# R loaded for two chunks at once and turned on TensorE into fp32, V and scaled A in one transposing transfer, and a new order of the work

## The chip, the cores and the metric

The kernel runs on one core of a Trainium2 chip. A core has a matrix engine (PE, TensorE, with a weight-load path PEld), a vector engine (DVE, VectorE), a scalar engine (ACT, ScalarE), a general engine (POOL, GpSimd), a queue that mostly issues transfers (SP, SyncE), and 16 DMA engines that all queues share. Operands lie in SBUF, results of PE in the banks of PSUM. The engines run side by side, each through its own instructions in program order, and wait for one another by semaphores. The metric is the time of one execution on the device in microseconds (us); less is better.

## The reference

Two layers. First a recurrence over 768 tokens for 4 x 8 heads of width 40, with a state of 40 x 40 for each head:

```python
for t in range(S):
    y[:, :, t] = np.einsum('bhd,bhde->bhe', rt, state)
    Sa = np.einsum('bhde,bhe->bhd', state, at)
    state_decay = state * wt[:, :, None, :] - np.einsum('bhd,bhe->bhde', Sa, bt)
    state = state_decay + np.einsum('bhd,bhe->bhde', vt, kt)
```

Then a feed-forward layer on the 3072 rows of 320 numbers that `y` makes: `h = x @ w_in` (320 x 2048), `g = max(h, 0) ** 2`, `out = g @ w_out` (2048 x 320). All inputs and the output are fp32.

## The kernel before, in words

**Tiling.** The 768 tokens are cut into 6 chunks of 128. One chunk of one sequence is a *batch*: 24 batches, number m = 4 x chunk + sequence, each with 128 tokens on the partitions and 8 heads x 40 columns. A batch has two *steps* of 4 heads (48 steps). Within a chunk the recurrence is written as matrix products: the decays are summed up (logarithm, a product with a triangle of ones, exponentials), K and B are divided by the summed decay, A is multiplied by it, and 128 x 128 products of tokens with tokens, masked to the past, take the place of the loop over tokens. A state (the tile UZ) goes from chunk to chunk. The feed-forward layer runs in 48 units over half-chunks (or, at both ends, over single batches) as their rows of `y` are done.

**Tokens of work.** The program is a string `ORDER` of some 1,900 tokens, one after the other; each names a function and a number, and often the engine (`:A` ACT, `:D` DVE, `:P` POOL) or the PSUM bank (`@f`). The order of the tokens is the order of issue on every engine and queue. The ones that matter here:

- `lW`, `lK`, `lB`, `lA`, `lV`, `lR` (`load`, L82 to L87): one input of one batch, 128 x 8 runs of 160 bytes, on SP's queue. R and V of a batch share a tile NRV; there are four such buffers (L64, L65).
- `ln`, `cs`, `cx`, `xi`, `gp`: the decays (L166 to L190). `pk` and `pa` (L201, L206) scale K and B, and A, into a padded bf16 tile of three planes, KBAp. `cv` (L210) casts R and V into a padded tile RVp. `gw` (L197) and `gl` make the chunk's last decay.
- *Turning*: products need K, B, A, R and V with the head's columns on the partitions. For batches 0 to 7 PE turns R and V (`rm`, L223, 8 transposes into a bf16 bank) and `rv` (L226) copies 1024 values of each partition out; `ta` and `at` do so for A. For batches 0 to 19 `kt` and `kv` turn K and B on PE. From batch 8 on, `rt` (L229) is a transposing transfer of R and V, and `ka` (L253) one of A (batches 8 to 19) or of K, B and A (20 to 23), all from SP's queue. Their targets are the tiles RV (four buffers) and KBT.
- `a` (L280): tokens-by-tokens products of K and B with A, in two halves of the array, into two banks; `av0`, `av1` mask them into CN. `p`, `m`, `k1`, `c`, `k2`, `s`: the correction of the recurrence. `t`, `tv`: the turned correction TB. `e` (L402): the products with R (from the tiles RV and TB); `ev0`, `ev1` mask them into EX. Where ACT evicts, POOL cuts the mask afterwards (`aq`, `eq`, L305).
- `z`, `kb` (L430, L444): `y` and the new state in one bank; `y` and `u` evict them. `xt`, `xv` turn `y` for the feed-forward layer. `x`, `jk`, `en` are sums for a check of the range (general code, not run on these inputs, stands behind it).
- `fr`, `fa`, `fb`: a unit's first product (L542); `ra`, `rb` relu on ACT (L562); `q` squares (L568); `o1`, `o2` the second product (L577); `ov`, `ow` evict and store.
- `wt`, `wd`, `wo`: the weights, from POOL's queue (`wd` on SP's). `f`, `i`: constants and zeros. `w` (`warm`, L134): filler products of 128 x 128 ones on PE, 26 for `w.0` and 8 for each other, 16 of the 19 in the first chunks and three at the end.

The queue of SP carries all loads, the transposing transfers and the stores in the string's order, and waits in line wherever one of them must wait.

## Time and profile before

| | |
|---|---|
| median of 3 runs | 257.62 us (256.45 to 258.14) |
| profiled execution, its own time | 259.12 us |
| its span, first to last instruction | 257.3 us |
| granted TensorE clock, mean | 0.993 |
| instructions | 9803 |
| transfers' packets | 184468, of these 180064 under 512 bytes |
| HBM read, written | 28.84 MB, 3.93 MB |

The page of the profile gives busy time by engine, the span in slices, the queues, the chain of waits that ended last (followed back from the last instruction), and groups of instructions by line. A windows view gives the busy time of each engine in a stretch. A matmul's duration in a group is from its start to its modelled end (some 220 ns for 128 columns); matmuls overlap, so the pace of a row of them is read from the chain, where eight turnings take 0.45 us. `hp`, `ca`, `ex`, `uy`, `tt`, `P`, `op_` are PSUM tiles, `hs`, `CN`, `EX`, `KBT`, `RV` tiles of SBUF.

### The profile page before, as it was taken

The numbers are of one execution on the slowest core, as the hardware profiler recorded it, in microseconds if no ns is written. First come the engines' busy times: TensorE is split into PE (matmuls) and PEld (weight loads), VectorE is DVE, ScalarE is ACT, GpSimd is POOL, SyncE is SP. The second block draws the span as 40 slices with busy tenths as digits, with TensorE's granted clock in tenths as the row PEclk, the third lists the DMA queues.
The fourth block names the chain that finished last, engine by engine and source line by source line (L and its number), as shares of the span: only waits on it lengthen the run. The fifth ranks groups of instructions, "written<-read, shape, count | busy, mean of one in ns | idle before, by whom it ended". The sixth has DMA issues, their size and how long they took to land.

```text
span 257.3 us, 9803 instructions
## 1 busy us (share of the span) xinstructions
PE 241.3 (94%) x4020; PEld 201.8 (78%) x4020; DVE 202.4 (79%) x429; ACT 205.9 (80%) x470; POOL 203.0 (79%) x231
## 2 busy tenths in 40 slices
PE   8897867999999999999999999999999997999993
PEld 7776656989888888788888788888878885787872
DVE  3887877899999889898798898879798986664440
ACT  3567989589989988978999887889989876869811
POOL 6487987779989979999998999897896993397110
PEclk9999999799999999999999999999999999999999
DMA  7999999999988989999999999989999989470011
GB/s 127 182 151 153 169 176 168 170 167 167 162 162 137 157 151 182 137 178 180 157 159 184 159 167 172 167 162 185 141 187 180 178 167 148 97 120 28 28 57 59
DMA packets 184468, 38.46 MB, mean 149 GB/s; under 512 B 180064, under 2 KB 183136, under 8 KB 184416
## 3 DMA queue, kind: packets, MB, share of 16 engines
q1 hardware_dynamic: 183072, 35.14, 80.9%
q0 software_dynamic: 1344, 2.62, 6.4%
q8 instruction: 33, 0.54, 0.9%
q14 instruction: 19, 0.16, 0.2%
HBM read 28.84 MB, written 3.93 MB: 127 GB/s over the span
## 4 chain that ended last, share of the span: by engine, by line
PE 58%; POOL 13%; DMA 12%; SPq 8%; ACT 4%; issue 2%; DVE 1%; POOLq 0%; ACTq 0%
PE hp L542 17%; SPq L85 8%; DMA NKB<-in_b_dram 6%; PE tt L218 3%; PE cs L173 3%; PE ca L287 3%; PE ex L410 3%; POOL Gt L568 3%; PE uy L456 3%; DMA NRV<-in_r_dram 2%; DMA KBT<-KBAp 2%; POOL KBAp L202 2%; PE uy L451 2%; PE P L344 2%; POOL CN L307 2%
## 5 line engine op out<-in xcount | busy, mean ns | idle before, releaser
L542 PE MATMUL hp<-XS,WIN 128*128 128x256 bf16 (+3 forms) x720 | 73.3, 255 | 0.0
L562 ACT ACTIVATE hs<-hp 128x512 bf16<-128x512 f32 x96 | 55.6, 600 | 14.5 <-PE hp L542 13.2
L542 PEld LDWEIGHTS <-WIN 128*128 128x128 bf16 (+1 forms) x720 | 49.6, 115 | 6.1 <-issue 3.6
L302 DVE TENSOR_TENSOR CN<-ca,MEX 128x512 bf16<-128x512 f32 x60 | 39.5, 683 | 8.6 <-PE ca L287 8.0
L577 PEld LDWEIGHTS <-Gt 128*128 128x128 bf16 x384 | 35.1, 97 | 12.2 <-issue 0.3
L302 DVE TENSOR_TENSOR EX<-ex,MEX 128x512 bf16<-128x512 f32 x60 | 39.8, 683 | 4.4 <-PE ex L410 4.3
L568 POOL TENSOR_TENSOR Gt<-hs 128x1024 bf16<-128x1024 bf16 x21 | 40.4, 1927 | 0.6 <-ACT hs L562 0.3
L307 POOL TENSOR_SCALAR_AFFINE_SELECT CN<-CN 128x512 bf16<-128x512 bf16 x36 | 25.1, 703 | 10.0 <-ACT CN L300 7.8
L307 POOL TENSOR_SCALAR_AFFINE_SELECT EX<-EX 128x512 bf16<-128x512 bf16 x36 | 25.0, 711 | 5.9 <-ACT EX L300 3.9
L198 POOL TENSOR_TENSOR Gp<-NW,GP 32x320 bf16<-32x320 f32 x20 | 17.6, 886 | 11.3 <-DVE osb L157 7.6
L568 DVE TENSOR_TENSOR Gt<-hs 128x1024 bf16<-128x1024 bf16 x27 | 21.7, 810 | 5.8 <-ACT hs L562 4.3
L365 ACT ACTIVATE jk<-CN 128x1024 bf16<-128x1024 bf16 x24 | 25.7, 1071 | 0.2
L300 ACT ACTIVATE CN<-ca 128x512 bf16<-128x512 f32 x36 | 21.0, 594 | 4.7 <-PE ca L287 4.5
L202 POOL TENSOR_TENSOR KBAp<-NKB,GI 128x640 bf16<-128x640 f32 x14 | 21.6, 1545 | 3.2 <-DMA NKB<-in_b_dram 2.5
L300 ACT ACTIVATE EX<-ex 128x512 bf16<-128x512 f32 x36 | 20.5, 597 | 2.8 <-PE ex L410 1.9
L287 PE MATMUL ca<-KBT 64*128 64x128 bf16 x384 | 18.2, 221 | 3.7 <-DMA KBT<-KBAp 1.7
L361 POOL TENSOR_TENSOR Cc<-x,SN 128x320 bf16<-128x320 f32 x24 | 20.1, 836 | 1.9
L456 PE MATMUL uy<-KBAp,EX 128*128 128x40 bf16 x384 | 21.3, 181 | 0.0
L207 POOL TENSOR_TENSOR KBAp<-NA,GP 128x320 bf16<-128x320 f32 x18 | 16.3, 907 | 5.6 <-DMA NA<-in_a_dram 2.9
L360 POOL TENSOR_TENSOR x<-Mc,c 128x320 f32<-128x320 bf16 x24 | 20.5, 854 | 0.3
L472 DVE TENSOR_TENSOR YN<-uy,GP 128x224 bf16<-128x224 f32 (+1 forms) x48 | 16.5, 346 | 4.4 <-PE uy L456 4.4
L456 PEld LDWEIGHTS <-EX 128*128 128x128 bf16 x384 | 17.9, 96 | 0.9 <-issue 0.3
(151 smaller groups left out, 623.0 us busy)
## 6 DMA issues: line engine op xcount, KB each, us to landing
NW<-in_w_dram SPq DMA_DIRECT2D x24, 160.0 KB, 3.8
NA<-in_a_dram SPq DMA_DIRECT2D x24, 160.0 KB, 4.0
NKB<-in_k_dram SPq DMA_DIRECT2D x24, 160.0 KB, 3.9
NKB<-in_b_dram SPq DMA_DIRECT2D x24, 160.0 KB, 4.3
NRV<-in_v_dram SPq DMA_DIRECT2D x24, 160.0 KB, 4.0
NRV<-in_r_dram SPq DMA_DIRECT2D x24, 160.0 KB, 3.9
out_dram<-osb SPq DMA_DIRECT2D x24, 160.0 KB, 3.4
WOUT<-in_moe_w_out_dram POOLq DMA_DIRECT2D x2, 640.0 KB, 6.6
```

Source lines behind the costliest of these rows:

```text
L85: nc.sync.dma_start(out=natural(pair, m)[:, u], in_=nat_srcs[key][bb, :, c * L:(c + 1) * L, :].rearrange("h t e -> t h e"))
L202: engine("pk", m).tensor_tensor(out=bt[m].KB[:, 0:2, :, 0:D], in0=nat.pop(("KB", m))[:], op=ALU.mult, in1=bt[m].GI[:].rearrange("p (u h) e ...
L287: nc.tensor.matmul(out=ca[s][:, i, u, :], lhsT=o.KBT[half(s), u, j0 + i, :], rhs=o.KBT[half(s), 2, j0 + i, :], start=(i == 0 and u == 0), ...
L300: nc.scalar.activation(out=out, in_=in_[:], func=ACTF.Copy)
L302: nc.vector.tensor_tensor(out=out, in0=in_[:], op=ALU.mult, in1=MEX[:].rearrange("p (i u) x -> p i u x", u=2))
L307: nc.gpsimd.affine_select(out=t_, in_=t_, pattern=[[0, 2], [0, 2], [1, L]], compare_op=ALU.is_gt, fill=0.0, base=0, channel_multiplier=-1)
L365: nc.scalar.activation(out=jk[:], in_=CNs[m, "b"][:].rearrange("p x i s u t -> p (x i s) u t")[:, :, 1, :], func=ACTF.Square, accum_out=AC ...
L456: nc.tensor.matmul(out=uy[:, (2 * i + s) * D:(2 * i + s + 1) * D], lhsT=EXs[st][:, i, s, u, :], rhs=o.KB[:, u, 2 * (j0 + i) + s, 0:D], sta ...
L542: nc.tensor.matmul(out=o.hp[u][:, i], lhsT=inner(g, rows, j), rhs=XSs[o.c][rows, g, o.bs, :], start=(o.begun[u] == 1), stop=(o.begun[u] > ...
L562: nc.scalar.activation(out=o.hs[:, u], func=ACTF.Relu, in_=o.hp[u][:].rearrange("p j a b -> p (j a b)"))
L568: engine("q", n).tensor_tensor(out=o.Gt[:, o.j0:o.j0 + 2 * o.per].rearrange("p j a b -> p (j a b)"), in0=hs, in1=hs, op=ALU.mult)
L577: nc.tensor.matmul(out=ops[n][:], rhs=WOUT[:, j, :], lhsT=Gts[h][:, b_, j, :] if h in SPLIT else Gts[h][:, j, b_, :], start=(j == 0), stop ...
```

## The change

- **R for two chunks.** Where the string has a `cr` token (batches 0 to 3 and 8 to 11), `lR` of these loads 256 tokens: partition p gets the tokens 2p and 2p+1 of two chunks, 128 x 8 runs of 320 bytes. `lR` of batches 4 to 7 and 12 to 15 is gone: 16 `lR` in place of 24. `cr` casts both chunks' R into plane 0 of two padded tiles, and `cv` of batches 0 to 15 casts V alone.
- **R turned on PE into fp32.** `rn` (16 tokens, batches 0 to 15) multiplies four 128 x 128 blocks with the identity into an fp32 bank, and `rv` (16) copies 512 fp32 values of each partition out and puts the even and odd tokens in order, into planes 0 and 3 of a tile RVT that now has four planes; plane 3 is the R of the odd chunk (`turned_r`). Batch m turns half of the heads for both chunks, batch m+4 the other half. `rm` is gone.
- **V and scaled A.** `pa` now writes plane 2 of the tile RVA (R, V, A) and not the tile of K and B. In batches 0 to 7 V is turned on PE alone (`vm`, four transposes; `vv` copies 512 bf16 values); A as before. In batches 8 to 15 one transposing transfer `rt` turns V and A together. In batches 16 to 19 `rt` turns R and V and a new `aa` A; in 20 to 23 there are `rt` (R, V), `aa` (A) and `ka` (K, B).
- **Fillers.** `warm` issues products of 512 columns, 7 for `w.0` and 2 for each other.
- **Order.** The whole string is written anew, 1937 tokens in place of 1909, with other engines for many of them. Counts that change: `q` 27 on DVE and 21 on POOL become 23 and 25; `pa` 6 on DVE and 18 on POOL become 8 and 16; `gw` 4 and 20 become 6 and 18; `pk` 10 and 14 become 11 and 13; `m` 15 on ACT and 9 on DVE become 11 and 13; `ov` 8 and 14 become 12 and 10; `s` 18 and 6 become 20 and 4; `kv` 6 and 14 become 8 and 12; `tv` 6 and 18 become 4 and 20; `at` 3 and 5 become 6 and 2; masks 72 on ACT and 120 on DVE become 70 and 122; `cv` 13 on ACT, 2 on DVE and 9 on POOL become 10, 4 and 10; `cr` 2, 1 and 5; `rv` 4 on ACT and 4 on DVE become 9 and 7; `vv` 5 and 3.

The diff, without the rest of the order and the table of tokens:

```diff
@@ -76,15 +76,25 @@
 
     def natural(key, m):
         if (key, m) not in nat:
-            nat[key, m] = natp.tile([128, len(key), NHH, D], FP32, name=f"N{key}", tag=f"N{key}")
+            tag = "NRV" if key == "RR" else f"N{key}"
+            nat[key, m] = natp.tile([128, len(key), NHH, D], FP32, name=tag, tag=tag)
         return nat[key, m]
+
+    def paired(m):
+        return ("cr", m - m // NB % 2 * NB) in pick
 
     def load(key, m):
         pair, u = SHARED.get(key, (key, 0))
         c, bb = divmod(m, NB)
-        nc.sync.dma_start(
-            out=natural(pair, m)[:, u],
-            in_=nat_srcs[key][bb, :, c * L:(c + 1) * L, :].rearrange("h t e -> t h e"))
+        if key == "R" and paired(m):
+            nc.sync.dma_start(
+                out=natural("RR", m)[:].rearrange("p a h e -> p (a h e)").rearrange(
+                    "p (h x) -> p h x", h=NHH),
+                in_=r[bb, :, c * L:(c + 2) * L, :].rearrange("h (p a) e -> p h (a e)", a=2))
+        else:
+            nc.sync.dma_start(
+                out=natural(pair, m)[:, u],
+                in_=nat_srcs[key][bb, :, c * L:(c + 1) * L, :].rearrange("h t e -> t h e"))
 
     NHC = 2 * NCH
     AN, AM, AC, AG, AI = 0, NBC, NBC + NHC, NBC + 2 * NHC, 2 * NBC + 2 * NHC
@@ -97,8 +107,10 @@
     MEX = gl.tile([128, 4, L], BF16, name="MEX")
     HM = gl.tile([128, 1, 2], BF16, name="HM")
     pads = {key: [gl.tile([128, len(key), NHH, 64], BF16, name=f"{key}p{i}") for i in range(n)]
-            for key, n in (("KBA", 4), ("G", 3), ("RV", 4))}
-    RVs = [gl.tile([128, 2, PB, L], BF16, name=f"RV{i}") for i in range(4)]
+            for key, n in (("KB", 4), ("G", 3))}
+    RVAs = gl.tile([128, 4, 3, NHH, 64], BF16, name="RVAp")
+    pads["RVA"] = [RVAs[:, i] for i in range(4)]
+    RVs = [gl.tile([128, 4, PB, L], BF16, name=f"RV{i}") for i in range(4)]
     SNs = [gl.tile([128, PB, 2, 64], BF16, name=f"SN{i}") for i in range(NSN)]
     UZs = [gl.tile([128, NP, 128], BF16, name=f"UZ{i}") for i in range(2)]
     YNs = [gl.tile([128, NG * 128], BF16, name=f"YN{i}") for i in range(3)]
@@ -114,7 +126,7 @@
             for u in range(2):
                 eng.memset(HM[64 * u:64 * u + 64, :, u:u + 1], 1.0)
         elif k < 16:
-            key, i = (("KBA", k - 5) if k < 9 else ("G", k - 9) if k < 12 else ("RV", k - 12))
+            key, i = (("KB", k - 5) if k < 9 else ("G", k - 9) if k < 12 else ("RVA", k - 12))
             eng.memset(pads[key][i][:] if key == "G" else pads[key][i][:, :, :, D:64], 0.0)
         elif k < 19:
             eng.memset(SNs[k - 16][:, :, :, D:64], 0.0)
@@ -131,10 +143,11 @@
     def bank(x, k, i=0):
         return HOME[pick[x, k][1][i]]
 
-    def warm(k, n=8):
-        wu = ps.tile([128, 128], FP32, name="wu", **bank("w", k))
-        for i in range(26 if k == 0 else n):
-            nc.tensor.matmul(out=wu[:], lhsT=ones_b[:], rhs=ones_b[:], start=True, stop=True)
+    def warm(k, n=2):
+        wu = ps.tile([128, 4, 128], FP32, name="wu", **bank("w", k))
+        for i in range(7 if k == 0 else n):
+            nc.tensor.matmul(out=wu[:], lhsT=ones_b[:], start=True, stop=True,
+                             rhs=ones_b[:].rearrange("p (u x) -> p u x", u=1).to_broadcast([128, 4, 128]))
 
     def half(s):
         return slice(64 * s, 64 * s + 64)
@@ -160,8 +173,13 @@
 
     def home(m):
         o = bt[m] = Batch()
-        o.G, o.KB, o.RV = (pads[key][m % len(pads[key])] for key in ("G", "KBA", "RV"))
+        o.G, o.KB, o.RV = (pads[key][m % len(pads[key])] for key in ("G", "KB", "RVA"))
         o.RVT, o.YN = RVs[m % 4], YNs[m % 3]
+        c, bb = divmod(m, NB)
+        o.both = bt[m - NB].both if c % 2 else Batch()
+        o.turned_r = lambda j: o.RVT[:, 3 if paired(m) and c % 2 else 0, j, :]
+        if c % 2 == 0:
+            o.both.pad = RVAs[:, 2 * (bb % 2):2 * (bb % 2) + 2, 0]
 
     def b_ln(m):
         bt[m].lnW = ffp.tile([128, NHH * D], FP32, name="lnW", tag="lnW", bufs=2)
@@ -204,11 +222,17 @@
             in1=bt[m].GI[:].rearrange("p (u h) e -> p u h e", u=1).to_broadcast([128, 2, NHH, D]))
 
     def b_pa(m):
-        engine("pa", m).tensor_tensor(out=bt[m].KB[:, 2, :, 0:D], in0=nat.pop(("A", m))[:, 0],
+        engine("pa", m).tensor_tensor(out=bt[m].RV[:, 2, :, 0:D], in0=nat.pop(("A", m))[:, 0],
                                       in1=bt[m].GP[:], op=ALU.mult)
 
     def b_cv(m):
-        move(pick["cv", m][0], bt[m].RV[:, :, :, 0:D], nat.pop(("RV", m))[:])
+        lo = 1 if paired(m) else 0
+        move(pick["cv", m][0], bt[m].RV[:, lo:2, :, 0:D], nat.pop(("RV", m))[:, lo:2])
+
+    def b_cr(m):
+        move(pick["cr", m][0], bt[m].both.pad[:, :, :, 0:D],
+             nat.pop(("RR", m))[:].rearrange("p a h e -> p (a h e)").rearrange(
+                 "p (h a e) -> p a h e", a=2, h=NHH))
 
     def turned(pad, us=(0, 1), t_=None, **place):
         if t_ is None:
@@ -220,17 +244,40 @@
                     in_=pad[:, u, 2 * j:2 * j + 2, :].rearrange("p a b -> p (a b)"))
         return t_
 
-    def b_rm(m):
-        bt[m].t1 = turned(bt[m].RV, **bank("rm", m))
+    def b_rn(m):
+        o, j0 = bt[m], 2 * (m // NB % 2)
+        o.t1 = ps.tile([128, 2, 2, L], FP32, name="tt", **bank("rn", m))
+        for j in range(2):
+            for a_ in range(2):
+                nc.tensor.matmul(
+                    out=o.t1[:, j, a_], rhs=IDb[:], start=True, stop=True, skip_group_check=True,
+                    lhsT=o.both.pad[:, a_, 2 * (j0 + j):2 * (j0 + j) + 2, :].rearrange(
+                        "p a b -> p (a b)"))
 
     def b_rv(m):
-        move(pick["rv", m][0], bt[m].RVT[:], bt[m].t1[:])
-
-    def b_rt(m):
+        o, j0 = bt[m], 2 * (m // NB % 2)
+        move(pick["rv", m][0],
+             o.RVT[:, 0:4:3, j0:j0 + 2, :].rearrange("p c j (t a) -> p j c t a", a=2),
+             o.t1[:].rearrange("p j a (c t) -> p j c t a", c=2))
+
+    def b_vm(m):
+        bt[m].t4 = turned(bt[m].RV, us=(1,), **bank("vm", m))
+
+    def b_vv(m):
+        move(pick["vv", m][0], bt[m].RVT[:, 1], bt[m].t4[:, 0])
+
+    def turn_by_transfer(m, lo, hi):
         o = bt[m]
         nc.sync.dma_start_transpose(
-            out=o.RVT[:].rearrange("p u j t -> p (u j) t"),
-            in_=o.RV[:].rearrange("p u h e -> p (u h e)"))
+            out=o.RVT[:, lo:hi].rearrange("p u j t -> p (u j) t"),
+            in_=o.RV[:, lo:hi].rearrange("p u h e -> p (u h e)"))
+
+    def b_rt(m):
+        lo = 0 if not paired(m) else 2 if ("vm", m) in pick else 1
+        turn_by_transfer(m, lo, 2 if ("aa", m) in pick or ("ta", m) in pick else 3)
+
+    def b_aa(m):
+        turn_by_transfer(m, 2, 3)
 
     def b_kt(m):
         bt[m].t2 = turned(bt[m].KB, **bank("kt", m))
@@ -238,23 +285,22 @@
     def kbt(m):
         o = bt[m]
         if not hasattr(o, "KBT"):
-            o.KBT = chp.tile([128, 3, PB, L], BF16, name="KBT", tag="KBT", bufs=4)
+            o.KBT = chp.tile([128, 2, PB, L], BF16, name="KBT", tag="KBT", bufs=4)
         return o.KBT
 
     def b_kv(m):
-        move(pick["kv", m][0], kbt(m)[:, 0:2], bt[m].t2[:])
+        move(pick["kv", m][0], kbt(m)[:], bt[m].t2[:])
 
     def b_ta(m):
-        bt[m].t3 = turned(bt[m].KB, us=(2,), **bank("ta", m))
+        bt[m].t3 = turned(bt[m].RV, us=(2,), **bank("ta", m))
 
     def b_at(m):
-        move(pick["at", m][0], kbt(m)[:, 2], bt[m].t3[:, 0])
+        move(pick["at", m][0], bt[m].RVT[:, 2], bt[m].t3[:, 0])
 
     def b_ka(m):
-        o, lo = bt[m], 2 if ("kt", m) in pick else 0
         nc.sync.dma_start_transpose(
-            out=kbt(m)[:, lo:3].rearrange("p u j t -> p (u j) t"),
-            in_=o.KB[:, lo:3].rearrange("p u h e -> p (u h e)"))
+            out=kbt(m)[:].rearrange("p u j t -> p (u j) t"),
+            in_=bt[m].KB[:].rearrange("p u h e -> p (u h e)"))
 
     def last_decay(m, uy, at):
         o = bt[m]
@@ -285,7 +331,7 @@
             for i in range(2):
                 for s in range(2):
                     nc.tensor.matmul(out=ca[s][:, i, u, :], lhsT=o.KBT[half(s), u, j0 + i, :],
-                                     rhs=o.KBT[half(s), 2, j0 + i, :], start=(i == 0 and u == 0),
+                                     rhs=o.RVT[half(s), 2, j0 + i, :], start=(i == 0 and u == 0),
                                      stop=True, skip_group_check=True)
 
     def st_a_ev(st, s):
@@ -324,7 +370,7 @@
         P = Ps[m] = ps.tile([128, PB, 2, 64], FP32, name="P", **bank("p", m))
         if c > 0:
             for j in range(PB):
-                nc.tensor.matmul(out=P[:, j, :, 0:D], lhsT=o.KBT[:, 2, j, :],
+                nc.tensor.matmul(out=P[:, j, :, 0:D], lhsT=o.RVT[:, 2, j, :],
                                  rhs=heads(UZ[:, PB * bb + j, :]), start=(j == 0), stop=False,
                                  skip_group_check=True)
         for h in range(NHH):
@@ -408,7 +454,7 @@
                 for s in range(2):
                     lhsT = SnT[half(s), j0 + i, :] if u else o.RVT[half(s), 1, j0 + i, :]
                     nc.tensor.matmul(out=ex[s][:, i, u, :], lhsT=lhsT,
-                                     rhs=o.RVT[half(s), 0, j0 + i, :],
+                                     rhs=o.turned_r(j0 + i)[half(s)],
                                      start=(i == 0 and u == 0), stop=True, skip_group_check=True)
 
     EXs = {}
@@ -432,7 +478,7 @@
         uy = uys[st] = ps.tile([128, 8 * D + PB], FP32, name="uy", **bank("z", st))
         if c > 0:
             for i in range(2):
-                nc.tensor.matmul(out=cols(uy, 2 * i * D), lhsT=o.RVT[:, 0, j0 + i, :],
+                nc.tensor.matmul(out=cols(uy, 2 * i * D), lhsT=o.turned_r(j0 + i),
                                  rhs=heads(TBs[st // 2 - NB + LAG][:, PB + j0 + i, :]), start=(i == 0), stop=False,
                                  skip_group_check=True)
             for i in range(2 if c + 1 < NCH else 0):
@@ -622,150 +668,153 @@
     SPLIT = (0, 1, 11)
     ORDER = """
-        f.1:D lW.0 f.2:P lA.0 w.4@x w.11@0 f.4:D lW.1 f.20:D f.0:D f.9:D w.8@u lK.0 ln.0 f.16:D
...
+        lW.0 lK.0 f.0:D f.13:D f.1:P w.13@1 ln.0 w.2@u f.3:D lW.1 f.14:P f.17:P f.20:D lV.0 f.5:D
...
     """
```

291 lines of the change are left out of this document (147 added, 144 removed).

## The prediction

> **What bounds the kernel now.** First the page's totals, then the stages, then the chain, then the groups. The page:
> ```profile
> PE 241.3 (94%) x4020; PEld 201.8 (78%) x4020; DVE 202.4 (79%) x429; ACT 205.9 (80%) x470; POOL 203.0 (79%) x231
> DMA  7999999999988989999999999989999989470011
> q1 hardware_dynamic: 183072, 35.14, 80.9%
> PE 58%; POOL 13%; DMA 12%; SPq 8%; ACT 4%; issue 2%; DVE 1%; POOLq 0%; ACTq 0%
> ```
> No engine is far ahead of the others, and the row of the 16 DMA engines reads 9 for most of the time. So an average decides nothing; the stages do (bounds; length, then busy us of PE, PEld, DVE, ACT, POOL; clock, DMA share, GB/s):
> ```profile
> 0.00:48.00 48.00, 39.02 (x678) 33.01 (x679) 36.52 (x84) 33.98 (x74) 34.79 (x56) 0.99 0.96 161
> 48.00:128.00 80.00, 79.91 (x1427) 68.32 (x1425) 71.78 (x149) 71.24 (x167) 74.31 (x80) 0.99 0.98 162
> 128.00:216.00 88.00, 87.01 (x1447) 72.11 (x1444) 75.94 (x158) 76.81 (x179) 78.19 (x81) 1.00 1.00 170
> 216.00:257.30 41.30, 35.38 (x480) 28.32 (x478) 18.17 (x42) 23.84 (x51) 15.75 (x17) 1.00 0.35 68
> 208.00:224.00 16.00, 14.16 (x226) 11.32 (x224) 10.75 (x21) 11.76 (x26) 7.68 (x10) 1.00 0.81 140
> ```
> The reader sees three regimes. Up to 48 us the DMA engines are full (0.96) while PE, whose 39.02 us hold fillers too, has gaps: the start waits for data. From 48 to 216 us PE is busy for 166.92 of 168 us with the DMA engines at 0.98 to 1.00 beside it: PE sets the pace, DMA is a close second, and DVE, ACT and POOL have 6 to 12 us to spare in each of the two stages. From 216 us PE runs nearly alone. The chain of waits shows where DMA still decides (start, length, what):
> ```profile
> 27.16 5.75 DMA NRV<-in_r_dram
> ...
> 36.12 7.58 DMA NKB<-in_b_dram
> 43.72 1.20 DVE KBAp L202
> 44.97 0.62 PE tt L218 x8
> ...
> 74.49 1.09 PE op__1912 L577 x8
> 75.91 0.45 PE tt L218 x8
> ...
> 131.54 3.66 DMA NKB<-in_b_dram
> 135.62 1.55 POOL KBAp L202
> ...
> 152.26 1.56 POOL KBAp L202
> 153.86 0.62 PE tt L218 x8
> ...
> 213.73 5.37 DMA KBT<-KBAp
> 219.54 0.50 PE uy L456 x16
> ```
> The start ends with batch 5's b and its turning. At 131.5 us a late b puts POOL behind, and the chain stays on POOL until 153.8. At 213.7 us the last chunk's scaled K and B leave for the transposing transfer late, and `a` waits for it.
>
> **The change part by part.** Prices, first of one instruction, from the groups kept apart by form (busy us, mean ns of one, idle before):
> ```profile
> L218 PE MATMUL tt<-IDb,RVp 128*128 128x128 bf16 x64 | 4.9, 219 | 0.1
> L137 PE MATMUL wu<-ones_b 128*128 128x128 bf16 x170 | 13.5, 242 | 1.1 <-DVE HM L113 1.1
> L153 ACT ACTIVATE RVp<-NRV 128x640 bf16<-128x640 f32 x13 | 9.6, 739 | 3.0 <-DMA NRV<-in_r_dram 3.0
> L155 POOL CAST RVp<-NRV 128x640 bf16<-128x640 f32 x9 | 6.8, 753 | 3.8 <-DMA NRV<-in_r_dram 2.5 <-PE cs L173 1.2
> L153 ACT ACTIVATE RV<-tt 128x1024 bf16<-128x1024 bf16 x4 | 4.1, 1019 | 0.0
> L157 DVE COPY RV<-tt 128x1024 bf16<-128x1024 bf16 x4 | 2.7, 680 | 0.0
> L157 DVE COPY KBT<-tt 128x512 bf16<-128x512 bf16 x5 | 2.1, 419 | 1.0 <-PE tt L218 1.0
> L153 ACT ACTIVATE KBT<-tt 128x512 bf16<-128x512 bf16 x3 | 1.8, 595 | 1.6 <-PE tt L218 1.6
> L302 DVE TENSOR_TENSOR EX<-ex,MEX 128x512 bf16<-128x512 f32 x60 | 39.8, 683 | 4.4 <-PE ex L410 4.3
> L300 ACT ACTIVATE EX<-ex 128x512 bf16<-128x512 f32 x36 | 20.5, 597 | 2.8 <-PE ex L410 1.9 <-issue 0.8
> L568 POOL TENSOR_TENSOR Gt<-hs 128x1024 bf16<-128x1024 bf16 x21 | 40.4, 1927 | 0.6 <-ACT hs L562 0.3
> L568 DVE TENSOR_TENSOR Gt<-hs 128x1024 bf16<-128x1024 bf16 x27 | 21.7, 810 | 5.8 <-ACT hs L562 4.3 <-issue 1.5
> ```
> Then of one issue on SP's queue, from the views of the tiles NRV, RV and KBT (min/median/max ns):
> ```profile
> L85 SPq DMA_DIRECT2D NRV<-in_r_dram x24: 429/638/1142, 9.8 to 218.9; - x24
> L231 SPq DMA_TRANSPOSE RV<-RVp x16: 1232/1378/2762, 85.8 to 224.9; - x16
> L255 SPq DMA_TRANSPOSE KBT<-KBAp x16: 1192/1417/2886, 72.5 to 213.7; - x16
> ```
> *PE.* `rm` goes: 8 batches of 8 turnings (the 64 of the first row). `vm` brings 8 x 4 and `rn` 16 x 4, together 96, so 32 more. The chain (at 75.91) gives 0.45 us for eight in a row, 56 ns each: **+1.8 us**, none of it in batches 0 to 7 (64 against 64), all in 8 to 15, where PE is the bound, so it counts in full. Bounds: 0 if it falls into PE's small waits, and 32 x 219 ns = 7.0 us if nothing overlaps; I take 1.8, because such turnings come in fours and eights. The fillers go from 170 of 128 columns to 43 of 512: 21,760 columns against 22,016, no change in time, and they fill waits.
>
> *Evictions.* Before, `rv` is 4 x 1.019 us on ACT and 4 x 0.680 on DVE. After, `rv` moves 512 fp32 values of each partition 16 times (9 on ACT, 7 on DVE) and `vv` 512 bf16 values 8 times (5 and 3). By the rows for such sizes: ACT 9 x 0.597 + 5 x 0.595 - 4.1 = +4.2, DVE 7 x 0.683 + 3 x 0.419 - 2.7 = +3.3. `rv` reads PSUM with a step of 128 and writes pairs; no row has that. Bounds: the bf16 rate (0.42 on DVE) and twice the fp32 rate (1.37); I take the fp32 rows, the nearest in size and type.
> The Trainium skill ("VectorE: DVE Perf Modes", section "Why PSUM operands drop a tier") speaks against fp32 here: VectorE reads fp32 from PSUM at single rate only, where bf16 may go at double rate. The rows bear it out (680 ns for 1024 bf16 values, 683 for 512 fp32). With bf16 the seven would cost 2.9 us and not 4.8, by this trace; off PE's path, either leaves the sum as it is.
>
> *Casts.* `cv` halves in 16 batches and `cr` takes the other half in 8 of double width: the same elements and 8 more instructions. A half cast costs between half and all of a whole one, so 0 to 16 x 0.37 = 6 us over three engines; I take 1, near the lower end, since halving a copy brings 680 ns to 419. With that and the letters that the new order gives (`q` on POOL 21 to 25 at 1.927 against 0.810 on DVE; `pa`, `gw`, `pk` the other way; `m`, `s`, `kv`, `tv`, `at`, `ov` between ACT and DVE), token for token by such rows, ACT has about 3, DVE 5 and POOL 3 us more than before. Their cover is the 6 to 12 us of each stage above: taken as **0**. If the cover is gone, each of these us counts, up to 5.
>
> *DMA and SP's queue.* 183,072 packets at 80.9% of 16 engines' 257.3 us are 18.2 ns each; a load of 128 x 8 runs is 1.16 us of all 16. Sixteen loads of R become eight with as many runs each, of 320 bytes. A run of double size costs between one and two of today's, so the eight save between 0 and 9.3 us; I take the middle, 4.6. In transposing transfers, batches 8 to 15 go from V, R and A in two to V and A in one; 16 to 19 keep two; 20 to 23 go from two to three (`rt`, `aa`, `ka`). That is 32 to 28 issues and 56 to 48 planes; taking 1,024 packets for each of the 144 loads and 128 for each of the 24 results, some 580 packets are left for a plane, so 8 planes are 5.3 us. DMA falls by about 10 us of 208, SP's queue by 8 x 0.64 + 4 x 1.4 = 10.7 us.
> The Trainium skill ("DMA: Bandwidth & Descriptors", section "Why small descriptors are slow (HBM only)") gives each packet a fixed 3 cycles beside one for every 32 bytes; by that rule (an estimate) 320 bytes cost 13 and two of 160 cost 16, so R would save 3.5 us and not 4.6.
> As PE is the pace from 48 us, the lighter queues buy only what DMA still ends:
> - Start: by the order, 35 loads stand ahead of `fr.0` before and after, but four of them are double: 0 to +4.7 us. Ahead of batch 5's `kt.5` they are 39 and 37: -2.3 to +2.3. In chunk 0 come four more `rn`, `rv` and the wide `cr`, on engines with 11 to 14 us free of 48. I take **+0.5**.
> - 131 to 154 us: the chain runs over POOL behind a b that was awaited 3.66 us. With SP's queue and DMA lighter by then, I take **-1.5** (0 to -3.7).
> - 208 to 224 us: PE does 14.16 of 16. The order now issues K and B of batch 23 over 90 places earlier, and `pk`, `pa` of 23 run on DVE. Late next is `aa.23` behind `ka.23` on SP, which stands 24 places ahead of `a.46` as `ka.23` did. For the 1.84 us that PE lacks, and a little of the small waits around, I take **-2.0** (0 to -5.4, the whole wait).
> - A new wait: `rt` of 8 to 15 waits for the cast of V and for scaled A, and behind it on SP stand loads and results. V gets later, A not; `e` needs V only after `a` needs A. **0**, bounds 0 to +3 (two issues of 1.4).
> - End: in the last units `q` runs on POOL (44, 45, 47: 1.93 against 0.81), beside seven lots of `o` of 1.09 us each on PE (the chain at 74.49): **0**, up to +1.1.
> Sum: 1.8 + 0.5 - 1.5 - 2.0 = -1.2 us. The profiled execution is 259.12 us with a span of 257.3, and 1.5 above the median of 257.62; so 257.9 for such an execution, and **256.4** beside the median.
>
> **The rivals.** About 1% (2.6 us) is what a measurement of this kernel can tell from no change.
> 1. The relief counts more. POOL has 78.19 of 88 us and leads the chain for 18 us after 135.6; DMA is at 1.00. If the late data of the middle and of the end go wholly, it is 257.6 + 1.8 - 3.7 - 5.4 = 250.4 with the rest at 0; halfway to there from the forecast is **253.4**. For it: DMA and SP are both lightened before 128 us. Against: PE is busy 79.91 of 80 where that happens.
> 2. The start shortens: two loads fewer ahead of `kt.5` save 2.3 us, or the dip of the clock goes, which the two rows below show: 0.04 and 0.07 of 16 us, 1.8 us. With one of them, 257.6 + 1.8 - 3.5 - 2.1 = **253.8**. Against: the double loads.
> ```profile
> 32.00:48.00 16.00, 12.11 (x263) 10.66 (x262) 13.01 (x32) 12.42 (x23) 11.57 (x18) 0.96 0.99 170
> 48.00:64.00 16.00, 16.00 (x334) 14.69 (x333) 14.57 (x31) 14.02 (x33) 13.84 (x16) 0.93 0.99 169
> ```
> 3. Slower, at the start: R for two chunks must be there, cast, turned and evicted before the first `e`. Where DMA is full, four double loads cost up to 4.7 us and four more evictions of some 0.65 in turn half of their 2.6, which later stages, bound by PE, cannot give back. It decides if the loads ahead of `fr.0` end last: 257.6 + 1.8 + 4.7 + 1.3 - 3.5 = **261.9**. Against: loads of chunk 1 are fewer by four.
> 4. Slower, evictions: ACT, DVE and POOL get 3 to 5 us each. If a bank is evicted late in the middle because `rv` stands ahead of a mask or a relu, PE waits: 257.6 + 1.8 + 5 - 3 (the other three terms) = **261.4**. It decides when the stage's DVE exceeds about 76 of 80 us.
> 5. It saves nothing that ends last: all transfers were hidden; PE's 1.8 stays, **259.4**.
>
> **How the numbers follow.** Forecast 256.4 (its own range 255.1 to 258.8) 0.27; rival 1 0.22; rival 2 0.10; rival 3 0.19; rival 4 0.14; rival 5 0.08. Faster by over 1% (below 255.0) is 1 and 2: 0.32. Within 1% is the forecast and 5: 0.35. Slower (above 260.2) is 3 and 4: 0.33. The range reaches from 252.0, halfway from rival 1 to its end, to 262.0, just over rival 3; beyond lie the strided eviction at double price and double PE prices.
>
> **What would show it.** Right: 96 turnings to `tt` of V and R with 56 ns each in a row, PE busy within 1 us of its length from 48 to 216 us, the DMA share there down by 0.03 to 0.06, no wait of `a` for a transposing transfer over 1 us near the end, evictions of R at 0.6 to 0.7 us. Wrong: the first `hp` later than before, PE below 77 of 80 us in the middle, a wait of `e` or `a` for the joint transfer, or evictions of R over 0.9 us. The new order moves every queue, and what it does to the small waits on PE no row of before shows; that is what most likely breaks this forecast.

## The result, and the profile after

The changed kernel took 259.37 us in the median (257.69 to 262.24, 22 runs) beside 257.69 us for the kernel before (255.48 to 260.4, 22 runs). The ratio is 1.0087, 95% interval 1.0060 to 1.0115: 2.2 us slower (1.5 to 3.0). Run again in a later round, as e11 below, it was 1.0038 (0.9998 to 1.0077). Weighted by their intervals the two give 1.007, or 1.8 us. A ratio leaves out, as slow, the runs over 1.5% above the fastest of the same kernel, which below takes three of e1's twelve runs and five of e7's; with all runs the ratios of the medians are 1.0076 and 1.0014. The profiled execution took 259.36 us with a span of 257.7, about its median; that of the kernel before was 1.5 us over its own, so the two spans, 257.3 and 257.7, differ by less than the medians do. The granted clock does not explain the loss: it was 0.994 in the mean of the changed kernel's 22 runs, and 0.990 to 0.993 in the runs of the kernel before beside the experiments below.

The page of the changed kernel, the lines that answer to the first fence of the prediction (busy time, DMA by slice, SP's packets, the chain by engine):

```profile
PE 243.3 (94%) x3925; PEld 195.3 (76%) x3925; DVE 207.9 (81%) x435; ACT 207.8 (81%) x482; POOL 203.2 (79%) x235
DMA  7999999999905997996999988988799985510011
q1 hardware_dynamic: 170528, 34.09, 76.1%
PE 64%; DVE 8%; DMA 8%; ACT 6%; SPq 5%; POOL 3%; issue 3%; POOLq 0%; DVEq 0%; ACTq 0%
```

The transfers did become lighter: 80.9% of 257.3 us were 208.2 us of all engines, 76.1% of 257.7 are 196.1, so 12 us less where the prediction had 10. But the DMA row now has a hole, 0 and 5 in the two slices from 71 to 84 us, where before it read 8. The stages of the changed kernel, as in the prediction, with the same columns:

```profile
0.00:48.00 48.00, 40.14 (x586) 28.01 (x588) 39.13 (x86) 37.53 (x86) 38.36 (x65) 0.96 1.04 175
48.00:128.00 80.00, 78.17 (x1415) 65.53 (x1410) 71.79 (x148) 68.92 (x165) 62.74 (x68) 1.00 0.87 154
128.00:216.00 88.00, 87.91 (x1428) 72.51 (x1426) 78.09 (x165) 74.75 (x179) 72.26 (x77) 1.00 0.98 162
208.00:224.00 16.00, 16.00 (x263) 12.90 (x261) 13.86 (x28) 12.52 (x31) 12.37 (x14) 1.00 0.69 138
64.00:80.00 16.00, 15.80 (x291) 13.26 (x289) 14.16 (x31) 14.27 (x36) 13.76 (x16) 1.00 0.53 99
80.00:96.00 16.00, 14.46 (x243) 11.75 (x241) 14.49 (x26) 12.56 (x26) 9.08 (x13) 1.00 1.06 173
```

Read the second column against the prediction's fence. From 208 to 224 us PE is busy for 16.00 us in place of 14.16: the stall at the end is gone. From 48 to 128 us it is busy for 78.17 of 80 in place of 79.91: a new stall came in the middle, and nearly all of it lies in 80 to 96 us, where the kernel before has this row:

```profile
80.00:96.00 16.00, 15.91 (x271) 13.48 (x270) 13.76 (x27) 14.79 (x34) 14.31 (x19) 1.00 0.88 148
```

So 1.45 us of busy time were lost at one place and 1.84 won at another. The waits of PE from 78 to 96 us in the changed kernel (line, what it waited for: sum, times, longest) name the place (the kernel before has no such wait there):

```profile
PE tt L242 <- DVE KBp L220: 1.3, 1, 1.3
PE ca L333 <- ACT RV L166: 0.3, 1, 0.3
```

That is `kt.8`, which turns K and B of batch 8 and needs `pk.8` on DVE. In the timeline (start, us, engine, line) DVE does this ahead of it:

```profile
78.52 0.85 DVE L225 TENSOR_TENSOR RVAp<-NA,GP 128x320 bf16<-128x320 f32 x1
79.30 2.03 DVE L614 TENSOR_TENSOR Gt<-hs 128x1024 bf16<-128x1024 bf16 x1
81.26 0.81 DVE L220 TENSOR_TENSOR KBp<-NKB,GI 128x640 bf16<-128x640 f32 x1
```

and POOL, at the same time:

```profile
78.99 1.80 POOL L220 TENSOR_TENSOR KBp<-NKB,GI 128x640 bf16<-128x640 f32 x1
```

The middle row of DVE is the square `q.6`. It took 2.03 us; of the 23 squares on DVE the fastest took 0.673 and the middle one 0.745. It ended 0.54 us after POOL's `pk.9`. The Trainium skill ("SBUF — State Buffer", section "SBUF: two separate sides") says that VectorE, in an instruction with two inputs in SBUF as this one, and GpSimd share one pair of ports as an exclusive lock, and that whoever starts second waits for the whole instruction of the other. By that rule (an estimate) the square would end 0.68 us after 80.79, having taken 2.17 us; the trace agrees within 0.14.

The hole in the transfers has another cause. SP's queue in the changed kernel, its longest wait for one instruction and the two issues around it:

```profile
SPq L271 <- POOL RVAp L225: 13.0, 2, 12.2
```
```profile
64.86 1.80 SPq L95 DMA_DIRECT2D NRV<-in_v_dram  x1
79.06 1.35 SPq L271 DMA_TRANSPOSE RV<-RVAp  x1
```

SP stood for 12.2 us at the joint transfer of batch 8, `rt.8`, until POOL had scaled A (`pa.8`), and seven loads stood behind it. (In e11, the same kernel once more, it stood for 6.2 us, and PE's wait for `pk.8` was 1.3 us all the same.) So there were two suspects, a queue that stood and a late scaling on DVE, beside PE's own 32 turnings.

### The profile page after: what moved, and what is told of

It reads as the page before. It is cut to its first block, busy times and chain, and to the rows that moved or that the text cites. A ratio compares the mean times of both kernels' runs of the same rounds, so it can differ in the third digit from the quotient of the medians.

```text
span 257.7 us, 9653 instructions
## 1 busy us (share of the span) xinstructions
PE 243.3 (94%) x3925; PEld 195.3 (76%) x3925; DVE 207.9 (81%) x435; ACT 207.8 (81%) x482; POOL 203.2 (79%) x235
## 3 DMA queue, kind: packets, MB, share of 16 engines
q1 hardware_dynamic: 170528, 34.09, 76.1%
## 4 chain that ended last, share of the span: by engine, by line
PE 64%; DVE 8%; DMA 8%; ACT 6%; SPq 5%; POOL 3%; issue 3%; POOLq 0%; DVEq 0%; ACTq 0%
PE hp L588 18%; SPq L95 4%; PE ex L456 4%; PE ca L333 3%; PE cs L191 3%; PE P L390 3%; PE uy L502 2%; PE tt L242 2%; DMA NRV<-in_r_dram 2%; DMA RV<-RVAp 2%; DMA NW<-in_w_dram 2%; DMA out_dram<-osb 2%; PE uy L497 2%; PE tb L434 1%; DVE EX L348 1%
## 5 line engine op out<-in xcount | busy, mean ns | idle before, releaser
L608 ACT ACTIVATE hs<-hp 128x512 bf16<-128x512 f32 x96 | 54.7, 601 | 11.6 <-PE hp L588 8.7
L614 POOL TENSOR_TENSOR Gt<-hs 128x1024 bf16<-128x1024 bf16 x25 | 47.9, 1916 | 7.7 <-ACT hs L608 7.5
L353 POOL TENSOR_SCALAR_AFFINE_SELECT CN<-CN 128x512 bf16<-128x512 bf16 x35 | 22.8, 663 | 14.9 <-ACT CN L346 12.9
L353 POOL TENSOR_SCALAR_AFFINE_SELECT EX<-EX 128x512 bf16<-128x512 bf16 x35 | 23.5, 678 | 4.7 <-ACT EX L346 4.0
L220 POOL TENSOR_TENSOR KBp<-NKB,GI 128x640 bf16<-128x640 f32 x13 | 20.8, 1603 | 6.7 <-DMA NKB<-in_b_dram 5.2
L502 PE MATMUL uy<-KBp,EX 128*128 128x40 bf16 x384 | 21.9, 182 | 0.0
L225 POOL TENSOR_TENSOR RVAp<-NA,GP 128x320 bf16<-128x320 f32 x16 | 14.4, 902 | 7.4 <-ACT GP L207 5.5
L333 PE MATMUL ca<-RV,KBT 64*128 64x128 bf16 x384 | 17.9, 217 | 1.9 <-DVE EX L348 1.2
L390 PEld LDWEIGHTS <-CN 128*128 128x128 bf16 x384 | 15.0, 96 | 5.2 <-issue 3.4
L191 PE MATMUL cs<-lnW,UTI 128*128 128x320 f32 x48 | 18.4, 465 | 0.3 <-ACT lnW L186 0.3
```

The source lines that it names most:

```text
L191: nc.tensor.matmul(out=cs[:].rearrange("p h e -> p (h e)"), lhsT=UTI[:], rhs=bt[m].lnW[:], start=True, stop=True)
L333: nc.tensor.matmul(out=ca[s][:, i, u, :], lhsT=o.KBT[half(s), u, j0 + i, :], rhs=o.RVT[half(s), 2, j0 + i, :], start=(i == 0 and u == 0), ...
L353: nc.gpsimd.affine_select(out=t_, in_=t_, pattern=[[0, 2], [0, 2], [1, L]], compare_op=ALU.is_gt, fill=0.0, base=0, channel_multiplier=-1)
L390: nc.tensor.matmul(out=Ps[m][:, h // 2, h % 2, 0:D], lhsT=CNs[m, "b"][:, h // 4, h // 2 % 2, h % 2, 1, :], rhs=X[:, h], start=False, stop= ...
L502: nc.tensor.matmul(out=uy[:, (2 * i + s) * D:(2 * i + s + 1) * D], lhsT=EXs[st][:, i, s, u, :], rhs=o.KB[:, u, 2 * (j0 + i) + s, 0:D], sta ...
L608: nc.scalar.activation(out=o.hs[:, u], func=ACTF.Relu, in_=o.hp[u][:].rearrange("p j a b -> p (j a b)"))
```

## The experiments

Theory A: the queue behind the joint transfer makes the loads late, and that costs the time. Theory A2: PE's idle 1.4 us ahead of `kt.8` is lost at full price. Theory B (rival 5 of the prediction): the transfers were hidden, nothing is saved, and PE's 1.8 us stay. Ratios are to the kernel before on the same chip, with 95% intervals. In each move of a token the token also leaves its old place.

**e1 to e3: the loads, and A scaled earlier.**

```diff
 e1
-        x.5 pa.8:P rt.8
+        x.5 pa.8:P lR.9 lR.8 lK.10 lK.11 lB.10 lB.11 lW.11 rt.8
 e2
-        x.4 cv.8:P m.7:D
+        cv.8:P pa.8:P x.4 m.7:D
 e3: both
```

> The changed kernel with seven loads (R of batches 9 and 8 with their pairs, K and B of 10 and 11, W of 11) moved ahead of the joint transfer of batch 8 on SP's queue; nothing else. Theory A, the queue behind the joint transfer: SP stood 12.2 us for scaled A of batch 8 with these loads behind it, and PE lost some 2 us in 80 to 96 us for it; then the time falls by 1.5 to 3 us against the changed kernel, to a ratio of 0.996 to 1.003 to the kernel before. Theory B, PE's pace: the loss is the 32 added turnings, the wait on SP is made good later; then the ratio stays at 1.006 to 1.011.

> The changed kernel with the cast of V and the scaling of A of batch 8 put ahead of the sums x of batch 4 (and so of 5) on POOL; the loads stay behind the joint transfer. Theory A: the queue of SP is freed some 3.6 us earlier out of 12, so about a third of the gain of moving the loads, 0.5 to 1 us against the changed kernel. Theory B: nothing, ratio 1.006 to 1.011. A third reading, that scaled A of batch 8 itself is what PE lacks and not the loads behind it: then this run gains more than moving the loads does.

> Both edits, loads ahead and scaled A first. Theory A: as moving the loads alone, with at most 0.5 us more, ratio 0.994 to 1.002. Theory B: ratio 1.006 to 1.011.

e1 gave 1.0021 (0.9975 to 1.0067), e2 1.0070 (1.0038 to 1.0102), e3 1.0017 (0.9982 to 1.0053). In e1 the hole was filled (a DMA share of 1.03 from 64 to 80 us), and yet:

```profile
80.00:96.00 16.00, 14.46 (x237) 11.74 (x236) 14.50 (x26) 12.62 (x27) 9.16 (x12) 1.00 0.73 132
```

PE lost the same 1.5 us there. So the hole in the transfers did not make that stall; whether the late loads cost something elsewhere, these intervals do not settle: e1 and e3 lie below the changed kernel, but overlap with it (e3 with e11 only), and `kt.8` still waited 1.3 and 1.1 us in them.

**e5: PE's price.** Twelve products of 128 columns that nobody reads, ahead of `kt` of each batch 8 to 15 of the kernel before.

```diff
+    def more(k):
+        wu = ps.tile([128, 128], FP32, name="wu", **bank("wx", k))
+        for i in range(12):
+            nc.tensor.matmul(out=wu[:], lhsT=IDb[:], rhs=IDb[:], start=True, stop=True)
```

> The kernel before with 96 more products of 128 columns on PE, 12 ahead of each turning of K and B of batches 8 to 15, whose results nobody reads; nothing is left out. If PE sets the pace there, each costs 56 ns in full: +5.4 us, ratio 1.021, and the 32 of the change cost 1.8. If PE has room in its small waits: under +2 us, ratio under 1.008, and the 32 cost under 0.7.

The ratio was 1.0200 (1.0151 to 1.0249), 5.2 us (3.9 to 6.4) for 96 products: 54 ns each (41 to 67), 1.7 us for 32 (1.3 to 2.1). The prediction's 56 ns and 1.8 us lie within. The granted clock of these runs was higher than that of the kernel before beside them (0.998 and 0.993 in the mean), which may hide part of the price.

**e6: lighter transfers alone.** The kernel before, with R of batches 8 to 23 loaded in runs of 1280 bytes. These are other values of R, so the computation differs.

```diff
+        if key == "R" and m >= 8:
+            nc.sync.dma_start(
+                out=natural(pair, m)[:, u].rearrange("p h e -> p (h e)"),
+                in_=r[bb].rearrange("h t e -> (h t e)")[c * L * NHH * D:(c + 1) * L * NHH * D].rearrange(
+                    "(p x) -> p x", p=128))
+            return
```

> The kernel before with R of batches 8 to 23 loaded as 128 runs of 1280 bytes in place of 1024 runs of 160 (other values of R, so the result is not the reference's): 16 loads whose packets cost some 1.16 us of all 16 engines each become short ones, about 9 to 14 us of transfer work less between 45 and 215 us, nothing else moved. Reading 1 (transfers are hidden behind PE from 48 us on, rival 5): ratio 0.998 to 1.002 and a DMA share of 0.90 to 0.94 in place of 0.98 to 1.00 there. Reading 2 (relief counts, as the terms of 1.5 and 2.0 us assumed): 1.5 us or more faster, ratio under 0.994.

The ratio was 0.9992 (0.9956 to 1.0029). Its row of 48 to 216 us, and SP's packets:

```profile
48.00:216.00 168.00, 165.62 (x2850) 138.88 (x2847) 145.69 (x302) 146.85 (x344) 154.00 (x160) 1.00 0.94 166
```
```profile
q1 hardware_dynamic: 168736, 35.14, 76.7%
```

Ten us of transfer work went (208.2 us to 76.7% of 258.3 = 198.1), the share in these stages fell from 0.99 to 0.94, and the time did not move. So a stage in which the transfers are at 0.99 and PE at 166.92 of 168 us is not bound by both: less transfer work bought nothing (a gain of over 1.2 us lies outside the interval), while more work on PE cost time in e5. PE's busy time did not rise either; in this row it is 1.3 us lower. SP had as many transfers to issue as before, so a shorter queue is not tested here.

**e12 and e9: what the stall at the end was worth.** e12 moves one lot of products of the kernel before on PE (`a.46`, and its eviction), behind work that is ready; e9 hurries the data instead.

```diff
 e12
-        s.22:A fr.38@fs a.46@u1 eq0.42 eq0.43 kb.43 ov.16:A av0.46:A eq1.42 kb.41 fb.38 en.35 y.41 t.22@x
+        s.22:A fr.38@fs eq0.42 eq0.43 kb.43 ov.16:A eq1.42 kb.41 fb.38 en.35 y.41 t.22@x a.46@u1 av0.46:A
 e9
-        lB.22 y.37
+        lB.22 lK.23 lB.23 y.37
-        fb.36 gw.23:D
+        fb.36 pk.23:D gw.23:D
-        e.41@f1 rt.21
+        e.41@f1 ka.23 rt.21
```

> The kernel before with one product moved on PE: a of unit 46 behind kb of 43 and 41, fb of unit 38 and t of batch 22, some 1.5 us of products, so that PE works while the last transposing transfer of K, B and A lands; no queue is touched. Reading 1 (the end wait was worth what PE lacked): the wait of 1.9 us shrinks to under 0.5 and the time falls by 1.4 to 1.9 us, ratio 0.993 to 0.995. Reading 2 (a of 46 leads the chain to the end, so that its lateness only moves on): PE's wait shrinks but the ratio stays within 0.998 to 1.003.

> The kernel before with the end of its chunk 5 issued earlier: loads of K and B of batch 23 some 90 places earlier, their scaling ahead of gw of 23 on VectorE, their transposing transfer ahead of rt of 21. Reading 1 (the end wait was worth what PE lacked there, the term of 2.0 us of the prediction): the wait of 1.9 us ahead of a of unit 46 goes and the time falls by 1.8 to 2.0 us, ratio 0.992 to 0.993. Reading 2 (the last units fill it later anyway, or rt of 21 comes late in turn): the wait goes but the ratio stays within 0.998 to 1.002.

e12 gave 0.9960 (0.9922 to 0.9998): 1.0 us faster (0.1 to 2.0), and the lowest median of all kernels here, 257.23 us. PE's waits from 208 to 224 us in the kernel before and in e12:

```profile
PE ca L287 <- DMA KBT<-KBAp: 1.7, 1, 1.7
```
```profile
PE xt L489 <- ACT CN L300: 0.7, 1, 0.7
PE ca L287 <- DMA KBT<-KBAp: 0.4, 1, 0.4
PE P L327 <- ACT hs L562: 0.3, 1, 0.3
```

Of 1.7 us, 1.3 went, and 1.0 came back as two smaller waits; PE was busy for 14.67 of these 16 us, 0.5 more than before. So neither reading is borne out as it stood: half a microsecond of idle time was removed, and a gain of 0.1 to 2.0 us agrees with its full price but does not measure that of the whole stall. The clock differed as well: 0.997 in the mean of e12's runs and 0.992 in those of the kernel before beside it, 1.2 us of the span at most. How much of the gain is the clock's stays open. e9 was a miss of mine: 1.0159 (1.0101 to 1.0217), slower. Its waits from 200 to 224 us:

```profile
PE uy L435 <- DMA RV<-RVp: 2.6, 1, 2.6
PE hp L542 <- DVE osb L157: 1.9, 1, 1.9
```

`ka.23`, placed ahead of `rt.21`, held SP's queue until 215.49, and the R and V of batch 21 came late. The stall was removed by making a larger one. So e9 prices nothing, and shows that one token in the wrong place of a queue can cost more than the stall it was to remove.

**e7, e7b, e8, e10, e15: the stall at 80 us removed.** All have `pk.8` ahead of `pa.9` and `q.6` on DVE. e8 adds e1's loads; e10 adds e2's `pa.8` as well; e15 also loads W of batch 16 earlier, by 43 places (its expectation says some 55).

```diff
 e7, e7b
-        q.7:D y.13 vv.7:A pa.9:D o2.1 q.6:D
+        q.7:D y.13 vv.7:A pk.8:D pa.9:D o2.1 q.6:D
 e15, beside e10's moves
-        ln.14 lA.13 rb.16
+        ln.14 lA.13 lW.16 rb.16
```

> The changed kernel with one token moved: the scaling of K and B of batch 8 (pk on VectorE) stands ahead of the scaling of A of batch 9 and of the square of unit 6 on VectorE. In the changed kernel that square takes 2.03 us, beside a scaling of K and B on GpSimd of 1.80 us, where most such squares take 0.68, and PE idles 1.4 us until kt of 8. Theory A2 (that idle is lost time): the 80 to 96 us stretch has PE busy 15.7 us or more in place of 14.46, and the time falls by 1.2 to 1.5 us, to a ratio of 1.003 to 1.004 of the kernel before. Theory B (PE's 1.8 us alone makes the result): PE fills that stretch but a later wait takes the gain back; the ratio stays at 1.007 to 1.009.

> The changed kernel with both moves: the seven loads ahead of the joint transfer of batch 8, and pk of batch 8 ahead of the square on VectorE. Theory A and A2 together (queue behind the joint transfer costs some 1.7 us, the late pk 1.4 us): ratio 0.995 to 0.999 of the kernel before, so the new order's losses are these two. Theory B: not under 1.003, since PE's 1.8 us of turnings stay whatever the queues do.

> The changed kernel itself once more, so that the next three have it beside them on the same chip. All theories: ratio 1.006 to 1.011 of the kernel before, as in the result.

> The changed kernel with pk of batch 8 first on VectorE, once more, beside the changed kernel on the same chip. The first run gave 0.996 and had PE idle 1.4 us less ahead of kt of 8, but PE's wait moved on, to the second product of unit 6 (0.64 us). Theory A2: 0.8 to 1.5 us under the changed kernel, ratio 1.003 to 1.006 of the kernel before. If the first run stands: 0.996, 3 us under the changed kernel, which no wait of PE seen in it would explain. Theory B: within 0.5 us of the changed kernel.

> The changed kernel with all three moves: pk of 8 first on VectorE, the scaling of A of batch 8 ahead of the sum x of step 4 on GpSimd, and the seven loads ahead of the joint transfer. With loads and pk alone the joint transfer left SyncE at 83.00 us, 1.2 later than without the loads, and PE waited 1.11 us for it ahead of a of unit 16. Theory A3 (the joint transfer must both come late on the queue for the loads and early for a): even with A scaled some 1.6 us earlier SyncE reaches the transfer only when seven loads are issued, at 82 to 83 us, PE still waits about 1 us there, and the ratio is 1.000 to 1.005. Rival: with A early all waits of that stretch go, PE is busy 15.5 us of 80 to 96, and the ratio is 0.993 to 0.998.

> The changed kernel with the three moves of before (pk of 8, A of 8, the seven loads) and the load of W of batch 16 some 55 places earlier. In three profiled runs of moved kernels ScalarE waited 2.0 to 2.4 us for this load near 131 us and PE idled 1.9 to 2.3 us behind it; in three others it did not. Theory D (data late by chance is what is left of the loss): the load is there in time in every run, the spread of the times narrows and the ratio is 0.994 to 0.999. Rival (PE's 1.8 us stay and nothing else is left): 1.001 to 1.005 as with the three moves alone, no narrower.

| run | ratio | 95% interval |
|---|---|---|
| e11, the changed kernel again | 1.0038 | 0.9998 to 1.0077 |
| e7 | 0.9960 | 0.9920 to 1.0001 |
| e7b, same chip as e11 | 1.0031 | 0.9989 to 1.0073 |
| e8 | 1.0032 | 0.9990 to 1.0075 |
| e10, same chip as e11 | 1.0019 | 0.9980 to 1.0057 |
| e15 | 1.0053 | 1.0017 to 1.0088 |

The wait of `kt.8` is gone in all five. In e8 another one took its place; its waits of PE from 78 to 96 us:

```profile
PE ca L333 <- DMA RV<-RVAp: 1.0, 1, 1.0
PE op__2122 L623 <- DVE osb L170: 0.5, 1, 0.5
PE ca L333 <- ACT RV L166: 0.3, 1, 0.3
```

There SP issued `rt.8` behind the seven loads only at 83.00 us, and `a.16` waited for scaled A. So here the joint transfer is a wait for PE, once the loads stand ahead of it. In e10, with `pa.8` earlier, that wait is gone too and PE is busy for 15.46 of 16 us:

```profile
80.00:96.00 16.00, 15.46 (x248) 12.78 (x247) 15.23 (x28) 13.35 (x29) 10.41 (x13) 1.00 0.90 129
```

The rival in e10's expectation was right on the waits and wrong on the time. The mean of the five ratios is 1.0019, that of the changed kernel 1.007: 0.5%, 1.3 us, less. It would be easy to read this as the worth of the stall, but the runs do not show it. e1, e3 and e14, which kept a wait of 1.0 to 1.3 us ahead of `kt.8`, lie as low (1.0021, 1.0017, 1.0024); e8 won no busy time of PE in this stretch (14.31 of 16 us, against 14.46); without e7, whose 0.996 did not stand, the mean is 1.0034; and on one chip e7b and e11 differ by 0.07% only. So these runs show that the wait can be removed, and leave open what that is worth. Theory D of e15 was a load of W that is late by chance: in e1, e7 and e7b ACT waited 2.0 to 2.4 us for it near 131 us, and PE 1.5 to 1.9 us behind ACT. It fell: in e15 the load came in time, but the ratio did not fall.

**e13: a dose.** Since removing 1.4 us is near what can be told apart, four more squares on DVE make the stall larger.

```diff
-        pa.9:D o2.1 q.6:D z.14@1
+        pa.9:D o2.1 q.6:D qx.6 z.14@1
+            "qx": lambda n: [f_q(n) for _ in range(4)],
```

> The changed kernel with the square of unit 6 done four more times on VectorE (same values), right behind the first and ahead of pk of batch 8: a dose. Each takes 0.68 us or more, so pk, and kt of 8 behind it on PE, come 2.7 to 4 us later. Theory A2 (PE idle there is lost time at full price): PE idles 2.7 to 4 us more in 80 to 96 us and the time rises by as much, to a ratio of 1.015 to 1.023. Rival (later slack gives it back, so the idle of 1.4 us was no cause of the result): ratio under 1.011.

The ratio was 1.0226 (1.0173 to 1.0280), 4.0 us over the 1.007 of the changed kernel (some 1.5 either way). PE's wait:

```profile
PE tt L242 <- DVE KBp L220: 4.2, 1, 4.2
```

So 2.9 us more of idle PE cost 2.5 us or more, and nothing later gave them back. Part of the 4.0 us may be the clock, which was 0.983 in the mean of e13's six runs and 0.994 in the changed kernel's 22. The two profiled executions, with clocks of 0.990 and 0.993, differ by 3.2 us (262.58 and 259.36), about the added wait. That the 1.3 us of the changed kernel count in full too is inferred from this dose; the runs that removed them could not measure them.

**e14: who slows the square.** `q.6` on POOL and `pk.9` on DVE.

```diff
-        q.6:D z.14@1 s.7:A fa.8 en.3 fr.8@fe fr.9@uf pk.9:P pk.8:D
+        q.6:P z.14@1 s.7:A fa.8 en.3 fr.8@fe fr.9@uf pk.8:D pk.9:D
```

> The changed kernel with two letters exchanged: the square of unit 6 on GpSimd and pk of batch 9 on VectorE, behind pk of 8. Theory C (the square took 2.03 us because GpSimd ran pk of 9 beside it): pk of 8 now starts some 2 us earlier on VectorE, kt of 8 waits under 0.3 us, PE is busy 15.5 us or more of 80 to 96, and the ratio is about that of the kernel with pk first, 0.998 to 1.004. Rival (VectorE was simply full there): the two scalings on VectorE come to as much as the square, and PE still idles 1 us or more.

The ratio was 1.0024 (0.9987 to 1.0061); `kt.8` still waited 1.0 us. DVE and POOL in e14:

```profile
78.07 3.25 DVE L220 TENSOR_TENSOR KBp<-NKB,GI 128x640 bf16<-128x640 f32 x2
```
```profile
77.75 2.15 POOL L614 TENSOR_TENSOR Gt<-hs 128x1024 bf16<-128x1024 bf16 x1
```

The two scalings took 3.25 us, where one alone takes 0.81: the first took 2.51 us and ended after the square on POOL, the second 0.81. The square is on the other engine, and now the scaling beside it is the slow one. Theory C holds in that the slowness belongs to the pair; its forecast that the wait would go was wrong for the same reason. The rival's forecast, that PE would still idle for 1 us or more, came true, but not for its reason: at 0.81 us each the two scalings would have come to 1.62 us, and the square had taken 2.03.

**e4: V and A in two transfers again.**

```diff
-        pa.8:P rt.8
+        pa.8:P rt.8 aa.8
...
```

> The changed kernel with the joint transposing transfer of V and A of batches 8 to 15 taken apart into one of V and, right behind it, one of A: the same planes, eight issues of some 1.25 us more on SyncE. Theory A (the queue stands at scaled A, wherever that stands): the same wait for scaled A of batch 8, SyncE has 10 us more to issue, and the ratio is 1.007 to 1.015, not better than the changed kernel. Rival (the joining itself costs, since V waits for A): V arrives earlier and the ratio falls under 1.004.

The ratio was 1.0136 (1.0079 to 1.0193), not better than the changed kernel, and above the 1.004 that the rival needed. So joining as such is not what cost the time. Whether eight more issues in SP's queue do is not shown: the interval overlaps with that of the changed kernel.

## Why the prediction was wrong, step by step

The forecast was 256.4 us, a sum of -1.2; measured was about +2 (1.5 to 3.0 in the first run). The time of rival 5, 259.4, came within 0.1 us, but by luck and another road: something was saved and something else lost. (The prediction's sum for rival 1 comes to 250.3 and not 250.4; nothing rests on it.)

- **PE, +1.8:** right. 54 ns each (41 to 67) in e5, +1.7.
- **Evictions, sizes:** right. The groups of the changed kernel have the durations that were taken from the masks, 0.597 and 0.683 us:

```profile
L166 ACT ACTIVATE RV<-tt 128x512 bf16<-128x512 f32 x9 | 5.2, 603 | 0.3 <-DVE RV L170 0.2
L170 DVE CAST RV<-tt 128x512 bf16<-128x512 f32 x7 | 4.8, 687 | 0.6 <-PE tt L252 0.6
```

- **Work on ACT, DVE and POOL, "taken as 0" under a cover of 6 to 12 us per stage:** this step failed. The amounts were right or high (by the pages DVE has 5.5 us more, ACT 1.9 and POOL 0.2, for 5, 3 and 3). But cover is not a sum over a stage. At 77 to 82 us the new order put `q.7`, `pa.9`, `q.6` on DVE beside `pa.8` and `pk.9` on POOL, all ahead of `pk.8`, and the two engines held each other up. PE lost 1.3 us there while DVE was free for 8 us of the 80 in that stage. The loss stands in the traces of the result and of e11; that it counts as time rests on e13's dose, since the runs that removed it could not tell. Rival 4 had named a late engine in the middle, with evictions as its cause and a price of 5 us.
- **131 to 154 us, -1.5:** this step failed too, and by the prediction's own rows. The prediction had PE busy for 87.01 of 88 us and still took 1.5 us from a chain over POOL; PE had other work all the while. The row of 128 to 160 us, of the kernel before and of the changed one, shows that PE could win 0.2 us there, and in e6 lighter loads of R bought no time either:

```profile
128.00:160.00 32.00, 31.79 (x531) 26.36 (x529) 28.18 (x61) 27.57 (x66) 30.68 (x31) 1.00 1.02 166
```
```profile
128.00:160.00 32.00, 31.96 (x508) 26.05 (x506) 28.40 (x61) 27.62 (x68) 27.61 (x30) 1.00 1.06 168
```

- **208 to 224 us, -2.0:** right, as far as the trace goes: PE 14.16 to 16.00 us, and no wait for the transfer is left. As time it was priced only in part, by e12's 0.5 us.
- **The new wait of `rt`, 0 (to +3):** the wait came, 12.2 us on SP, and was hidden from PE in the changed kernel; e8 shows it at 1.0 us on PE as soon as the queue is arranged otherwise. In e11 SP's wait was 6.2 us. Its cost through late loads is between 0 and some 1.3 us (e1, e3 against the changed kernel) and stays open.
- **Start, +0.5:** not taken apart by any run, but the traces are near it. The first `hp` came at 41.9 us where it came at 40.1 before, which the prediction named as a sign against it; in all 13 traces with the new start it came at 41.9 to 43.7, in the five with the old one at 39.9 to 41.6. Fillers left out, PE had 43 products more left at 48 us in the mean of the 13 than in that of the five. The change itself adds 32 of these; the other 11 are 0.6 us at 54 ns, an estimate, since the products differ in width.

With 1.7 for PE, 1.3 at 80 us, -0.2 and -1.8 for the later stages by PE's rows, and the start at the forecast's 0.5, the sum is +1.5 us: at the lower end of the first run's interval, inside e11's (0 to 2.0). The two failed steps, 1.3 each, are 2.6 of the 2.7 us from -1.2 to +1.5. Of this sum only PE's term was measured as time by itself; the 1.3, the -0.2 and the -1.8 are idle time of PE in traces, so the account is worked out in this part and not measured.

## What to carry to other kernels

Ask of every saving whether PE (or whatever sets the pace) was idle at that place: here a chain of waits that ran over another engine for 20 us was worth no more than the idle time of PE beside it. Cover has to be read at the place where a result is needed, not as spare time of a stage: look at what stands ahead of that one instruction on its engine, and at what POOL does while DVE works (and the other way round). Before an instruction that waits is put on a queue, list what stands behind it, as e9 shows; but moving the rest ahead of it makes the waiting instruction itself late, as e8 shows.
